# Attention start and emission order of a fused attention and two-layer feed-forward kernel: rms_g by rows, batch 0's softmax in halves, fill products by a sliding span, a seeded plan

## The chip, the cores and the metric

The kernel runs on one core of a Trainium2 chip. The metric is the device time of one launch in microseconds (us), as the median of several runs. Engine names are those of the profile: PE is TensorE's matrix products, PEld its weight loads, DVE is VectorE, ACT is ScalarE, POOL is GpSimd, SP is the queue that issues most transfers. L557 is line 557 of the kernel before.

## The reference

The inputs are q, k, v of shape (4, 8, 576, 64), phi of shape (4, 8, 576, 32), and the weights of two feed-forward blocks; the weights are float64 and are taken apart bit by bit in the kernel. All results are float32-accurate.

```
a   = exp(phi - max over the 576 positions);  a /= sum over the positions + 1e-9
k_m = a^T k ;  v_m = a^T v                     # per batch and head, 32 x 64
p   = softmax(q k_m^T / 8) ;  x = p v_m        # 2304 tokens x 512
xn  = x / sqrt(mean(x*x) + 1e-6) * rms_g
h   = (silu(xn @ w_gate) * (xn @ w_val)) @ w_out          # 512 -> 1536 -> 512
out = act2(h @ w_in) @ w_out2                             # 512 -> 2048 -> 512
```

## The kernel before, in words

The kernel has three stages that overlap. First comes the attention over four batches. For each batch `soft` finds the maximum of phi over the positions, subtracts it and takes the exponential, and sums it; `memory` then contracts that with k and v (L578), divides by the sum (L597 is the product that adds the sums over the partitions, L607 to L624 the division) and transposes the small result (L632, L641: kmT, which the scores read). `pair` makes the scores (L694) and the softmax for two groups of 128 tokens at a time. Second comes the first feed-forward block: 24 pieces of 512 KB of the float64 weights are loaded to tiles called raw (L310) and converted to float32 by some five operations on DVE, ACT and POOL (`convert`, L310 to L346); `vw` folds v_m into them (L905), `gv` makes gate and value (L955), `out1` contracts with w_out (L1050). Third comes the second block as a fast matrix product with seven sub-products (L1393 and L1516).

In `soft` the maximum is found as follows. `fold` halves the nine position groups by four operations (L500); a transpose on PE (L513) and a reduction on DVE (L518) give two columns of maxima, `gm`. DVE then multiplies the identity by them (L523, tile `dg`), and PE multiplies `dg` by a matrix of ones, `spread` (L530), so that every partition holds the maxima. DVE subtracts them from phi (L536, one operation on 1152 columns), and ACT takes the exponential (L543, one operation). For the sum, `fold` is called again, this time on POOL. Its scratch tile `half` has one buffer for all folds.

The loads of phi, k, v and q all go out from SP (L442, L449, L477), in the order of the list LOADS: phi and kv of batch 0, q of batch 0, phi and kv of batch 1, and so on. rms_g, 512 values, is loaded by POOL (L415) to the tile gT with one value per partition and column, so every value is a piece of 4 bytes. gT is read when a batch's v_m is scaled (L647).

The order of all instructions is written by a planner, the class `Agenda`. Each stream of work (a generator) yields steps with an engine and a duration in us that is written in the code, for example `yield "V", 1.35`. The planner keeps a model clock, always takes the step that can start first (ties go to the lower priority number), and emits its instruction. On the chip each engine runs its instructions in the emitted order. The model times thus decide the order, nothing else.

`heat` emits products of zeros (bf16, 512 columns, L557) on PE, which the code calls heat and this document fill products. Their planned duration is 0.2133 us each. Before, the planner counts PE's work in fixed ticks of 3.413 us and adds fill products late in each tick until the tick holds 2.09 us; one bank, number 4, is theirs, and they end once the exponential of batch 2 is done, `('e', 2)`.

Of the kernel before, what the change touches and what calls it, by code (L numbers as in the profile page):

```python
# [1 line left out]

# [12 lines left out]
P = 128  # L15
# [21 lines left out]

HEAT = (4, ('e', 2), 2.09, 0.34)

# [10 lines left out]
FETCH = (256, 63, 80.0, 6.1, 3.6, 80)  # L50
TICK = 3.413
WARM = 1.38
P_SOFT, P_PAIR, P_CONV, P_VW, P_GV, P_OUT1, P_W2, P_F2 = 0, 100, 800, 102, 850, 900, 3000, 4000
# [10 lines left out]
class Agenda:  # L64
# [11 lines left out]
    def __init__(self, room):  # L76
        self.room = dict(room)
        self.turn = {}
        self.ticks = {}
        self.flags = {}  # L80
        self.free = {"D": 1.7}
        self.given = {}
        self.issued = 5
        self.landed = {}
        self.now = 0.0
        self.port = 0.0
        self.done = 0.0
        self.live = []
        self.count = 0

# [14 lines left out]
    def _landed(self, n):  # L105
        return self.landed.get((n + FETCH[1]) // FETCH[0] - 1, 0.0)

    def _issue(self, n, at, t):
# [20 lines left out]
    def _start(self, x):  # L129
        kind, arg = x[3]  # L130
        at = x[4]
        if kind == "take":
            return (at, None) if self.room[arg] else None
        if kind == "pick":
            free = [z for z in arg if self.room["bank", z]]
            return (at, min(free, key=lambda z: self.given.get(z, 0.0))) if free else None
        if kind == "flag":
            return (max(at, self.flags[arg]), None) if arg in self.flags else None
        if kind in ("give", "rest"):
            return at, None  # L140
        if kind == "heat":
            at = max(at, self.free.get("P", 0.0), self._landed(self.issued))
            tick = int(at / TICK)
            need = HEAT[2] - self.ticks.get(tick, 0.0)
            if need <= 0:
                return (tick + 1) * TICK + 0.01, None
            slow = 1.0 if self.ticks.get(tick - 1, 0.0) > WARM else 2.0
            return max(at, (tick + 1) * TICK - (need + HEAT[3]) * slow), None
        times = arg if isinstance(arg, tuple) else (arg,)
        if kind[0] == "P":  # L150
            at = max(at, self._landed(self.issued))
        starts = [max(at + HOP.get(x[5] + e, HOP[e]), self.free.get(e, 0.0)) for e in kind[: len(times)]]
        bias = BIAS.get(kind, 0.0)
        took = [self._took(kind, e, t, s) for e, t, s in zip(kind, times, starts)]
        z = min(range(len(times)), key=lambda z: starts[z] + took[z] + (bias if z else 0.0))
        return starts[z], z

    def run(self, stop=None):
        while self.live and not (stop and stop in self.flags):
# [28 lines left out]
            elif kind == "heat":  # L188
                tick = int(at / TICK)
                value = self.ticks.get(tick, 0.0) < HEAT[2]  # L190
                if value:
                    slow = 1.0 if self.ticks.get(tick - 1, 0.0) > WARM else 2.0
                    self.ticks[tick] = self.ticks.get(tick, 0.0) + arg
                    done = at + arg * slow
                    done += self._issue(2, at, arg * slow)
                    self.free["P"] = done
            else:
                value = kind[z]
                t = self._took(kind, value, arg[z] if isinstance(arg, tuple) else arg, at)
                if value == "P":  # L200
                    tick = int(at / TICK)
                    slow = 1.0 if self.ticks.get(tick - 1, 0.0) > WARM else 2.0
                    self.ticks[tick] = self.ticks.get(tick, 0.0) + t * DUTY.get(kind.rstrip("0123456789"), 1.0)
                    t *= slow
                    t += self._issue(int(kind.lstrip("Pmsw")), at, t)
                done = self.free[value] = at + t
# [9 lines left out]
def tile_attn_moe(tc, q, k, v, phi, w_gate, w_val, w_out1, rms_g, w_in2, w_out2, out):  # L216
# [85 lines left out]
    def convert(src, pieces, dst, split, done, place=None):  # L302

        yield "take", "raw"
        yield "D", D_HALF
        n = nconv[0]
        nconv[0] += 1
        raw = wv.tile([P, CU, 2], U32, tag="raw", name=f"raw{n}", bufs=BUFS["raw"])
        rs = raw.rearrange("p n t -> p (n t)")
# [37 lines left out]
        yield "give", "raw"  # L347
        if split:
            if place:
# [77 lines left out]
    def loads():  # L427

        for s in LOADS:
# [8 lines left out]
            if s[0] == "phi":  # L438
                b = s[1]
                yield "Dq", 1.8  # L440
                t = phi_t[b] = ld.tile([P, 4, J, M], F32, tag="phi", name=f"phi{b}", bufs=BUFS["phi"])
                nc.sync.dma_start(out=t.rearrange("p c j m -> p c (j m)"), in_=by_half(phi[b], J * M))  # L442
            elif s[0] == "kv":
# [28 lines left out]
    def load_q(s):  # L472
        b = s[1]
        yield "take", "q"
        yield "Dq", 3.6
# [12 lines left out]
    def fold(name, x, to, op):  # L488

        kind, e, took = ("Vmax", nc.vector, (0.67, 0.4, 0.3, 0.3)) if op == ALU.max else (  # L490
            "G", nc.gpsimd, (1.24, 0.8, 0.48, 0.48)
# [3 lines left out]
        for n, (dst, y, z) in enumerate((  # L495
# [4 lines left out]
            e.tensor_tensor(out=dst, in0=y, in1=z, op=op)  # L500
        yield "give", "half"

    def soft(b):
# [19 lines left out]
        nc.vector.tensor_tensor(  # L523
            out=dg, in0=ident.unsqueeze(1).to_broadcast([P, 2, P]),
            in1=gm.unsqueeze(2).to_broadcast([P, 2, P]), op=ALU.mult,
        )
# [8 lines left out]
        yield "V", 1.35  # L535
        nc.vector.tensor_tensor(  # L536
            out=ph, in0=ph,
            in1=mv.rearrange("p (c m) -> p c m", m=M).unsqueeze(2).to_broadcast([P, 4, J, M]),
            op=ALU.subtract,
        )  # L540
        yield "give", m_bank
        yield "A", 1.16
        nc.scalar.activation(out=ph, in_=ph, func=AF.Exp)  # L543
        mark(("e", b))
# [3 lines left out]
        mark(("s1", b))  # L548

    def heat():  # L550

        yield "take", ("bank", HEAT[0])
        t = psum.tile([P, 512], F32, tag=f"b{HEAT[0]}", name="heat")
        while HEAT[1] not in agenda.flags:
            go = yield "heat", 0.2133
            if go:
                nc.tensor.matmul(  # L557
                    out=t.rearrange("p (x n) -> p x n", x=2), lhsT=zeros[:, 0:P],
                    rhs=zeros.unsqueeze(1).to_broadcast([P, 2, 256]), start=True, stop=True,
                    skip_group_check=True,  # L560
                )
        yield "give", ("bank", HEAT[0])

    s1_t = {}

    def memory(b):
# [6 lines left out]
        for j in range(J):  # L573
            yield "Pm32", 0.25
            for g in range(2):
# [17 lines left out]
        yield "flag", ("s1", b)  # L593
        yield "P8", 0.1
        for g in range(2):
# [42 lines left out]
        for z in range(2):  # L638
# [5 lines left out]
            )  # L644
        mark(("km", b))
        yield "V", 0.28
        nc.vector.tensor_tensor(  # L647
# [39 lines left out]
    def scores(pr, qT, scv, w):  # L687
        if pr[0] < B:
            for i in range(2):
                yield "Ps32", 0.65  # L690
                for c in range(2 * i, 2 * i + 2):
# [8 lines left out]
            return  # L700
        yield "Ps64", 0.85
        for c in range(4):
# [14 lines left out]
    def pair(n):  # L717
# [107 lines left out]
        y = st.tile([P, I], F32, tag="y", name=f"y_{name}", bufs=BUFS["e"])  # L825
        yield "G", 0.4
        nc.gpsimd.tensor_scalar(
# [50 lines left out]
    def vw():  # L878
# [7 lines left out]
        for group in VW:  # L886
# [11 lines left out]
            for z, (n, hi, lo, vps) in enumerate(got):  # L898
                yield "Pw64", 1.02 if z + 1 < len(got) else 1.25
                t = w_t.pop(n)  # L900
# [273 lines left out]
    order.enter_context(tc.manual_schedule())  # L1174
    add(0, loads())
    for b in range(B):
        add(P_SOFT + 2 * b, soft(b))
# [461 lines left out]
```

## Time and profile before

| | us |
|---|---|
| median of 3 runs | 775.58 |
| lowest and highest run | 775.37, 775.75 |
| the profiled execution, whole | 775.85 |
| its span in the trace | 774.1 |

Times in the trace are us from the start of the span. 1.75 us of the profiled execution lie around its span. In the views by stretches, `(x39)` is the number of instructions, PEclk the granted TensorE clock as a share of full speed, and the DMA share is the mean busy share of the core's 16 DMA engines (packets that overlap count twice, so it can pass 1). "issue" as a reason for a wait means that the profile shows nothing that was waited for.

### The profile page before, as it was taken

To read this page: it belongs to the slowest core of one execution; us is meant where nothing else is said; L and a number is where in the kernel's file an instruction comes from. 1 tells how busy PE (TensorE), PEld (TensorE's weight loads), DVE (VectorE), ACT (ScalarE), POOL (GpSimd) and SP (SyncE) were. 2 spreads that over 40 slices of the span, in tenths; PEclk is the share of its full clock that TensorE was granted. 3 is DMA by queue.
4 is the path that set the end of the run, shared out by engine and by line. 5 is a ranking of instruction groups with operands and counts; after the bars stand their busy time and mean duration, and the time that the engine had idled before them with its cause. 6 is when DMAs were issued, how large, how long until landed. Compare 5 with 4: busy or idle time off the path is not lost.

```text
span 774.1 us, 17215 instructions
## 1 busy us (share of the span) xinstructions
PE 759.8 (98%) x6383; PEld 701.4 (91%) x6383; DVE 618.9 (80%) x1250; ACT 466.5 (60%) x967; POOL 65.6 (8%) x89
## 2 busy tenths in 40 slices
PE   8999999999999999999999999999999999999997
PEld 4777798889889988988899999999999999999997
DVE  3799789998888776767788889985599895689963
ACT  1678877865565655646466668555476463565552
POOL 3546700000000000000000000000000000000000
PEclk9999999999999999999999999999999999999999
DMA  9994537788688765599547898888888878858875
GB/s 326 377 372 146 202 121 241 240 264 290 232 271 284 262 232 204 213 322 317 196 164 250 301 311 294 248 278 286 279 267 269 269 237 256 266 178 243 272 245 180
DMA packets 113395, 197.49 MB, mean 255 GB/s; under 512 B 10400, under 2 KB 41120, under 8 KB 113312
## 3 DMA queue, kind: packets, MB, share of 16 engines
q1 hardware_dynamic: 112896, 196.06, 76.2%
q8 instruction: 51, 0.84, 0.4%
q10 hardware_dynamic: 384, 0.33, 0.1%
q14 instruction: 32, 0.26, 0.1%
q0 software_dynamic: 32, 0.00, 0.1%
HBM read 151.26 MB, written 45.09 MB: 254 GB/s over the span
## 4 chain that ended last, share of the span: by engine, by line
PE 91%; DVE 4%; ACT 3%; issue 1%; POOL 1%; DMA 0%; DVEq 0%; POOLq 0%; ACTq 0%
PE ops L1050 19%; PE acc_b L1516 15%; PE qb L1393 13%; PE gps L955 10%; PE vps L955 10%; PE qc L1393 6%; PE acc_c L1516 6%; PE qa L1393 3%; PE vwps L905 3%; PE xp L815 1%; PE heat L557 1%; PE qps L743 1%; PE kvps L578 1%; DVE gg_A L1466 1%; ACT raw L328 1%
## 5 line engine op out<-in xcount | busy, mean ns | idle before, releaser
L1050 PE MATMUL ops<-ab,wo1h 128*128 128x512 f32 (+1 forms) x480 | 137.7, 372 | 0.2 <-ACT xs L1064 0.2
L1393 PE MATMUL qb<-xop,wr 128*128 128x384 f32 x576 | 111.1, 338 | 0.0
L1393 PEld LDWEIGHTS qb<-xop,wr 128*128 128x128 f32 x576 | 100.7, 188 | 0.3 <-ACT u L1355 0.3
L1050 PEld LDWEIGHTS ops<-ab,wo1h 128*128 128x128 f32 x480 | 84.7, 189 | 16.4 <-issue 3.7
L1050 PE MATMUL ops<-ab,wo1l 128*128 128x512 f32 (+1 forms) x240 | 88.5, 369 | 0.0
L1516 PE MATMUL acc_b<-wor,gg_A 128*128 128x256 f32 x648 | 79.6, 280 | 1.4 <-ACT gg_A L1464 0.8
L1516 PEld LDWEIGHTS acc_b<-wor,gg_A 128*128 128x128 f32 x648 | 78.2, 188 | 1.8 <-ACT gg_A L1464 1.0
L1355 ACT ACTIVATE u<-qb 128x384 f32<-128x384 f32 x72 | 35.1, 488 | 55.6 <-PE qb L1393 55.2
L1393 PE MATMUL qc<-xop,wr 128*128 128x384 f32 x288 | 58.3, 337 | 0.0
L1516 PE MATMUL acc_c<-wor,gg_S 128*128 128x256 f32 x432 | 53.0, 280 | 0.0
L1050 PEld LDWEIGHTS ops<-ab,wo1l 128*128 128x128 f32 x240 | 45.3, 189 | 7.8
L1516 PEld LDWEIGHTS acc_c<-wor,gg_S 128*128 128x128 f32 x432 | 52.2, 188 | 0.0
L1516 PE MATMUL acc_b<-wor,gg_S 128*128 128x256 f32 x432 | 52.0, 280 | 0.0
L1516 PEld LDWEIGHTS acc_b<-wor,gg_S 128*128 128x128 f32 x432 | 51.6, 188 | 0.0
L1393 PEld LDWEIGHTS qc<-xop,wr 128*128 128x128 f32 x288 | 50.9, 188 | 0.0
L328 ACT ACTIVATE raw<-raw 128x512 uint32<-128x512 uint32 x68 | 45.4, 672 | 0.0
L987 ACT ACTIVATE kvth<-gps 128x64 f32<-128x64 f32 (+2 forms) x100 | 29.0, 304 | 22.2 <-PE gps L955 21.7
L1021 ACT ACTIVATE ab<-kvth 128x512 fp32r<-128x512 f32 (+1 forms) x40 | 22.5, 566 | 30.6 <-PE ops L1050 30.6
L955 PE MATMUL gps<-late,vwh 128*128 128x288 f32 x192 | 39.6, 295 | 0.0
L955 PE MATMUL vps<-late,vwh 128*128 128x288 f32 x192 | 39.6, 295 | 0.0
L1026 DVE TENSOR_TENSOR ab<-kvth,ab 128x512 fp32r<-128x512 f32 (+1 forms) x39 | 24.9, 640 | 17.3 <-ACT ab L1021 17.1
L925 DVE TENSOR_TENSOR vwl<-vwps,vwh 128x512 fp32r<-128x512 f32 x48 | 32.5, 686 | 6.5 <-ACT vwh L923 6.5
(185 smaller groups left out, 1741.8 us busy)
## 6 DMA issues: line engine op xcount, KB each, us to landing
wr<-win_d SPq DMA_DIRECT2D x168, 256.0 KB, 3.7
wor<-wout_d SPq DMA_DIRECT2D x168, 256.0 KB, 3.3
raw<-in_moe_w_out_dram SPq DMA_DIRECT2D x28, 512.0 KB, 4.2
win_d<-wins SPq DMA_DIRECT2D x56, 256.0 KB, 4.2
wout_d<-wouts SPq DMA_DIRECT2D x56, 256.0 KB, 2.5
raw<-in_moe_w_in_dram SPq DMA_DIRECT2D x16, 512.0 KB, 5.2
raw<-in_moe_w_gate_dram SPq DMA_DIRECT2D x12, 512.0 KB, 5.1
raw<-in_moe_w_val_dram SPq DMA_DIRECT2D x12, 512.0 KB, 5.2
```

The costliest lines, as they stand in the source:

```text
L328: nc.scalar.activation(out=low, in_=low, func=AF.Copy, scale=LOW_SCALE, bias=LOW_BIAS)
L557: nc.tensor.matmul(out=t.rearrange("p (x n) -> p x n", x=2), lhsT=zeros[:, 0:P], rhs=zeros.unsqueeze(1).to_broadcast([P, 2, 256]), start=T ...
L905: nc.tensor.matmul(out=vps[g][0][32 * c : 32 * c + 32, 2 * P * x : 2 * P * x + 2 * P], lhsT=vT[n // NF1 * 2 + x][hs, c, :], rhs=t[hs, c].r ...
L925: nc.vector.tensor_tensor(out=lv, in0=vps[g][0], in1=hv.bitcast(F32), op=ALU.subtract)
L955: nc.tensor.matmul(out=p[:, 0:HB], lhsT=wt[:, g, i, :], rhs=at[b][:, g, c], start=(g == 0 and y == 0), stop=(g == 1 and y == 2),)
L987: nc.scalar.activation(out=t, in_=g[:, c], func=AF.Silu)
L1021: nc.scalar.activation(out=ah, in_=src, func=AF.Copy)
L1026: (nc.vector if eng == "V" else nc.gpsimd).tensor_tensor(out=al, in0=src, in1=ah.bitcast(F32), op=ALU.subtract)
L1050: nc.tensor.matmul(out=p[:, 0:n], lhsT=wt[:, fc, d], rhs=at, start=(fc == 0 and x == 0), stop=(fc == NF1 - 1 and x == 2),)
L1355: nc.scalar.activation(out=u, in_=src, func=AF.Copy)
L1393: nc.tensor.matmul(out=bank, lhsT=wt[:, kc, :], rhs=xt[:, kc, :], start=(start and kc == 0 and i == 0), stop=(kc == 1 and i == 2), skip_gr ...
L1516: nc.tensor.matmul(out=acc[x + "001"[t]][:, t % 2], lhsT=g[:, gi, P * t : P * t + P], rhs=w[:, wi], start=((o, t) in FIRST and q == 0 and ...
```

## The change

It does seven things.

1. rms_g is loaded to four rows of 128 values (`g4`), from ACT's queue, and a new stream `gains` transposes it on PE after the exponential of batch 0, and copies it to gT by DVE. `memory` waits for that before it scales v_m.
2. k of batch 0 is issued from ACT's queue instead of SP's.
3. `dg` and `spread` go. The product that spreads the maxima takes `gm`, broadcast to 64 columns, as its weights and the identity as its moving operand.
4. For batch 0 the subtraction and the exponential are done in two halves, so that the first exponential can start after the first half; the sum's fold of batch 0 is on DVE instead of POOL.
5. Fill products: the planner keeps a list of PE's work, and adds a fill product when the 3.413 us that end after it hold less than 2.0 us of work. They end with kmT of batch 3, `('km', 3)`, and each takes the bank that is free and was given back first.
6. Each planned duration is multiplied by a random factor between 0.97 and 1.03 from a seeded generator.
7. Several planned durations are changed, and a raw load waits in the plan until the buffer four loads earlier is given back.

```
-HEAT = (4, ('e', 2), 2.09, 0.34)
+HEAT = (('km', 3), 2.0, 0.2133, (4, 5, 6, 7, 0, 1, 2, 3))
+SEED, WOBBLE = 4, 0.06
+    def _active(self, end):
+        total, start = 0.0, end - TICK
+        for a, b, work in reversed(self.active):
+            if b <= start:
+                break
+            total += work * (min(b, end) - max(a, start)) / (b - a) if a < end else 0.0
+        return total
         if kind == "heat":
             at = max(at, self.free.get("P", 0.0), self._landed(self.issued))
-            tick = int(at / TICK)
-            need = HEAT[2] - self.ticks.get(tick, 0.0)
-            if need <= 0:
-                return (tick + 1) * TICK + 0.01, None
-            slow = 1.0 if self.ticks.get(tick - 1, 0.0) > WARM else 2.0
-            return max(at, (tick + 1) * TICK - (need + HEAT[3]) * slow), None
+            while self._active(at + HEAT[2]) >= HEAT[1]:
+                at += 0.1
+            free = [z for z in HEAT[3] if self.room["bank", z]]
+            return (at, min(free, key=lambda z: self.given.get(z, 0.0))) if free else None
...
                 t = self._took(kind, value, arg[z] if isinstance(arg, tuple) else arg, at)
+                t *= 1 + WOBBLE * (self.random() - 0.5)
...
     def convert(src, pieces, dst, split, done, place=None):
         yield "take", "raw"
-        yield "D", D_HALF
         n = nconv[0]
         nconv[0] += 1
+        if n >= BUFS["raw"]:
+            yield "flag", ("raw free", n - BUFS["raw"])
+        yield "D", D_HALF
...
-    nc.gpsimd.dma_start(out=gT, in_=rms_g.rearrange("(c p) -> p c", p=P))
+    g4 = st.tile([KC, P], F32, name="g4")
+    nc.scalar.dma_start(out=g4, in_=rms_g.rearrange("(c p) -> c p", p=P))
-    spread = st.tile([P, HP], F32, name="spread")
-    nc.gpsimd.memset(spread, 1.0)
...
                 for i, src in ((0, k), (1, v)):
-                    yield "Dq", 3.6
-                    nc.sync.dma_start(
+                    yield "Dq", 3.0 if b == 0 else 3.3
+                    (nc.scalar if (b, i) == (0, 0) else nc.sync).dma_start(
...
-        kind, e, took = ("Vmax", nc.vector, (0.67, 0.4, 0.3, 0.3)) if op == ALU.max else (
+        kind, e, took = ("Vmax", nc.vector, (0.67, 0.4, 0.3, 0.3)) if op == ALU.max or name == "s0" else (
             "G", nc.gpsimd, (1.24, 0.8, 0.48, 0.48)
...
+    def exp_phi(b, c, n):
+        yield "A", 0.12 + 0.26 * n
+        nc.scalar.activation(out=phi_t[b][:, c : c + n], in_=phi_t[b][:, c : c + n], func=AF.Exp)
+        mark(("e", b, c))
...
-        yield "Vdg", 0.42
-        dg = st.tile([P, 2, P], F32, tag="dg", name=f"dg{b}", bufs=BUFS["gm"])
...
-                out=mv[HP * g : HP * g + HP], lhsT=spread, rhs=dg[:, g], start=True, stop=True,
+                out=mv[HP * g : HP * g + HP], lhsT=gm[:, g : g + 1].to_broadcast([P, HP]), rhs=ident, start=True, stop=True,
...
+        n = 2 if b == 0 else 4
+        for c in range(0, 4, n):
+            yield "V", 0.08 + 0.318 * n
...
+            add(P_SOFT, exp_phi(b, c, n))
...
+    def gains():
+        yield "flag", ("e", 0)
+        gp, g_bank = yield from bank("t", "gps")
+        yield "P2", 0.1
+        nc.tensor.transpose(gp[:, 0:KC], g4, ident[0:KC, 0:KC])
+        yield "V", 0.2
+        nc.vector.tensor_copy(out=gT, in_=gp[:, 0:KC])
+        yield "give", g_bank
+        mark("gT")
```

The changed planned durations are: the phi load 1.8 to 1.6; k, v and q 3.6 to 3.0 (batch 0's k and v) or 3.3; L578 0.25 to 0.22; L597 0.1 to 0.35; L694 0.65 to 0.5 and L705 0.85 to 1.0; L905 1.02 and 1.25 to 0.9 and 1.1; L827 0.4 to 0.3.

## Rows read from the trace of the kernel before

**Rows 1.** The page, part 1: busy us of each engine, share of the span, instructions
```profile
PE 759.8 (98%) x6383; PEld 701.4 (91%) x6383; DVE 618.9 (80%) x1250; ACT 466.5 (60%) x967; POOL 65.6 (8%) x89
```

**Rows 2.** Busy time of the engines in six stretches: us, PE, PEld, DVE, ACT, POOL
```profile
0.00:12.30 12.30, 10.86 (x39) 4.16 (x39) 3.94 (x8) 2.45 (x2) 4.15 (x20) 1.00 0.86 285
12.30:37.40 25.10, 23.05 (x500) 18.32 (x500) 16.88 (x45) 13.47 (x28) 12.53 (x16) 1.00 1.06 383
37.40:92.00 54.60, 49.40 (x814) 39.95 (x816) 48.48 (x108) 46.03 (x101) 34.29 (x41) 1.00 0.68 236
92.00:200.00 108.00, 108.00 (x995) 95.62 (x987) 96.52 (x202) 74.94 (x174) 7.80 (x9) 1.00 0.71 234
200.00:700.00 500.00, 499.21 (x3486) 474.34 (x3471) 399.61 (x784) 296.03 (x597) 6.87 (x5) 1.00 0.78 257
700.00:740.00 40.00, 39.20 (x333) 39.03 (x332) 37.06 (x76) 20.63 (x41) 0.00 (x0) 1.00 0.82 258
```

**Rows 3.** The same view, PE's fill products alone
```profile
0.00:12.30 12.30, 10.49 (x34) 1.00 0.86 285
12.30:37.40 25.10, 3.28 (x12) 1.00 1.06 383
37.40:92.00 54.60, 0.38 (x1) 1.00 0.68 236
```

**Rows 4.** Timeline of the first 21 us: start, us, engine and line
```profile
6.21 0.29 DVE L500 TENSOR_TENSOR pm<-pm,phi 128x128 f32<-128x128 f32 x1
8.06 0.27 PE L513 MATMUL mps<-ident,pm 128*128 128x128 f32 x1
8.37 0.29 DVE L518 TENSOR_REDUCE gm<-mps 128x2 f32<-128x128 f32 x1 [1.87 <-PE mps L513]
9.25 0.44 PE L530 MATMUL mps<-dg,spread 128*64 128x128 f32 x4
9.74 1.35 DVE L536 TENSOR_TENSOR phi<-phi,mps 128x1152 f32<-128x1152 f32 x1 [0.54 <-PE mps L530]
11.13 1.16 ACT L543 ACTIVATE phi<-phi 128x1152 f32<-128x1152 f32 x1 [5.10 <-DVE phi L536]
12.35 2.25 PE L578 MATMUL kvps<-kv,phi 64*32 64x128 f32 x144 [0.39 <-ACT phi L543]
12.38 1.28 POOL L500 TENSOR_TENSOR halfs<-phi 128x512 f32<-128x512 f32 x1 [7.49 <-ACT phi L543]
15.03 0.69 DVE L500 TENSOR_TENSOR halfm<-phi 128x512 f32<-128x512 f32 x1 [3.94 <-POOL s L500]
16.09 0.39 PE L597 MATMUL kvps<-consts,s 64*128 64x1 f32 x4 [0.96 <-POOL s L500]
20.28 0.38 ACT L641 ACTIVATE kmT<-kT 64x256 f32<-64x256 f32 x1
```

**Rows 5.** DMA issues by window of issue: KB each, us to landing
```profile
phi<-in_phi_dram SPq DMA_DIRECT2D x1, 576.0 KB, 3.9
kv<-in_v_dram SPq DMA_DIRECT2D x1, 1152.0 KB, 9.9
gT<-in_moe_rms_g_dram POOLq DMA_DIRECT2D x1, 2.0 KB, 6.9
kv<-in_v_dram SPq DMA_DIRECT2D x1, 1152.0 KB, 15.1
```

**Rows 6.** Timeline of the queues: when three of these were issued
```profile
0.72 0.46 SPq L442 DMA_DIRECT2D phi<-in_phi_dram  x1
1.77 0.51 SPq L449 DMA_DIRECT2D kv<-in_v_dram  x1
8.29 1.57 SPq L449 DMA_DIRECT2D kv<-in_v_dram  x1
```

**Rows 7.** Busy time in stretches of 1 us; the last number is GB/s
```profile
6.00:7.00 1.00, 1.00 (x5) 0.36 (x4) 0.47 (x2) 0.03 (x1) 0.00 (x0) 1.00 1.49 315
7.00:8.00 1.00, 1.00 (x6) 0.52 (x5) 0.00 (x0) 0.00 (x0) 0.00 (x0) 1.00 0.60 161
```

More of the change, by code (lines that the diff above doesn't have):

```diff
@@ L1 @@
 from contextlib import ExitStack
+from random import Random
 import concourse.bass as bass
@@ L83, in __init__ @@
         self.issued = 5
+        self.active = []
         self.landed = {}
@@ L88, in __init__ @@
         self.live = []
+        self.random = Random(SEED).random
         self.count = 0
@@ L189, in run @@
                 tick = int(at / TICK)
[L190 to L196, printed above, removed]
+                value = z
+                slow = 1.0 if self.ticks.get(tick - 1, 0.0) > WARM else 2.0
+                self.ticks[tick] = self.ticks.get(tick, 0.0) + arg
+                done = at + arg * slow
+                self.active.append((at, done, arg))
+                done += self._issue(2, at, arg * slow)
+                self.free["P"] = done
             else:
@@ L204, in run @@
                     t *= slow
+                    self.active.append((at, at + t, t * DUTY.get(kind.rstrip("0123456789"), 1.0)))
                     t += self._issue(int(kind.lstrip("Pmsw")), at, t)
@@ L347, in convert @@
         yield "give", "raw"
+        mark(("raw free", n))
         if split:
@@ L439, in loads @@
                 b = s[1]
-                yield "Dq", 1.8
+                yield "Dq", 1.6
                 t = phi_t[b] = ld.tile([P, 4, J, M], F32, tag="phi", name=f"phi{b}", bufs=BUFS["phi"])
@@ L474, in load_q @@
         yield "take", "q"
-        yield "Dq", 3.6
+        yield "Dq", 3.3
         t = q_t[b] = st.tile([P, 4, J, D], F32, tag="q", name=f"q{b}", bufs=BUFS["q"])
@@ L520, in soft @@
         )
-        yield "Vdg", 0.42
-        dg = st.tile([P, 2, P], F32, tag="dg", name=f"dg{b}", bufs=BUFS["gm"])
[L523 to L526, printed above, removed]
         yield "P8", 0.3
@@ L534, in soft @@
         yield "give", "gm"
[L535 to L540, printed above, removed]
+        n = 2 if b == 0 else 4
+        for c in range(0, 4, n):
+            yield "V", 0.08 + 0.318 * n
+            nc.vector.tensor_tensor(
+                out=ph[:, c : c + n], in0=ph[:, c : c + n],
+                in1=mv.rearrange("p (c m) -> p c m", m=M)[:, c : c + n].unsqueeze(2).to_broadcast([P, n, J, M]),
+                op=ALU.subtract,
+            )
+            add(P_SOFT, exp_phi(b, c, n))
         yield "give", m_bank
-        yield "A", 1.16
-        nc.scalar.activation(out=ph, in_=ph, func=AF.Exp)
+        for c in range(0, 4, n):
+            yield "flag", ("e", b, c)
         mark(("e", b))
@@ L548, in soft @@
         mark(("s1", b))
-    def heat():
[L552 to L562, printed above, removed]
+    def gains():
[7 more added lines that the diff above has]
+        mark("gT")
+    def heat():
+        while HEAT[0] not in agenda.flags:
+            z = yield "heat", 0.2133
+            t = psum.tile([P, 512], F32, tag=f"b{z}", name="heat")
+            nc.tensor.matmul(
+                out=t.rearrange("p (x n) -> p x n", x=2), lhsT=zeros[:, 0:P],
+                rhs=zeros.unsqueeze(1).to_broadcast([P, 2, 256]), start=True, stop=True,
+                skip_group_check=True,
+            )
     s1_t = {}
@@ L573, in memory @@
         for j in range(J):
-            yield "Pm32", 0.25
+            yield "Pm32", 0.22
             for g in range(2):
@@ L593, in memory @@
         yield "flag", ("s1", b)
-        yield "P8", 0.1
+        yield "P8", 0.35
         for g in range(2):
@@ L645, in memory @@
         mark(("km", b))
+        yield "flag", "gT"
         yield "V", 0.28
@@ L689, in scores @@
             for i in range(2):
-                yield "Ps32", 0.65
+                yield "Ps32", 0.5
                 for c in range(2 * i, 2 * i + 2):
@@ L700, in scores @@
             return
-        yield "Ps64", 0.85
+        yield "Ps64", 1.0
         for c in range(4):
@@ L825, in pair @@
         y = st.tile([P, I], F32, tag="y", name=f"y_{name}", bufs=BUFS["e"])
-        yield "G", 0.4
+        yield "G", 0.3
         nc.gpsimd.tensor_scalar(
@@ L898, in vw @@
             for z, (n, hi, lo, vps) in enumerate(got):
-                yield "Pw64", 1.02 if z + 1 < len(got) else 1.25
+                yield "Pw64", 0.9 if z + 1 < len(got) else 1.1
                 t = w_t.pop(n)
@@ L1175, in tile_attn_moe @@
     add(0, loads())
+    add(P_SOFT, gains())
     for b in range(B):
```

## Prediction

> **What bounds the kernel now.** I read the page's busy shares first: PE is busy for 759.8 of the 774.1 us of the span [rows 1], so the end moves only with PE's idle time, with work that PE does in vain, or with slower products. The second view cuts the span into stretches [rows 2] and shows where the idle time is: 1.44 us up to 12.3, 2.05 up to 37.4, 5.20 up to 92, nothing from 92 to 200, 0.79 from 200 to 700, 0.80 from 700 to 740. The third view takes the fill products out of the busy time [rows 3]: 10.49 us up to 12.3, 3.28 up to 37.4, 0.38 up to 92, 14.15 in all. So before 92 PE does no useful work for 8.69 + 14.15 = 22.8 us, and after 92 it is a queue that never runs dry. Whatever the change gains, it must gain before 92, by making that queue start earlier; after 92 it can save at most the 1.6 us just listed, and it can lose more.
>
> The fourth view is the timeline of the first 21 us, read as a chain [rows 4]. phi of batch 0 lands at 0.72 + 3.9 = 4.62 [rows 5, 6]; the maximum's fold ends at 6.50; its transpose starts only at 8.06, behind the twenty fill products that the plan put ahead of it; the reduction ends at 8.66, the spreading product starts at 9.25, the subtraction at 9.74, the exponential ends at 12.29. k and v need 2.25 us from 12.35, and then PE waits: the sum, folded on POOL from 12.38, lets L597 start only at 16.09. kmT is complete at 20.66, and the scores follow. The fold for batch 1 starts at 15.03, released by that same POOL sum, since both use the one `half` tile.
>
> Up to 37.4 the DMA engines are full (share 1.06) [rows 2]. From 37.4 to 92 DVE is busy 89% and ACT 84%: there the attention and the weight conversion share two engines, and this backlog sets when PE's queue is full.
>
> **The change, part by part.**
>
> *The head of batch 0, up to the exponential.* The transpose stays at 8.06: worked by hand from the code, the new fill rule plans twenty products ahead of it again (nine at the planner's slow rate up to 3.84, then eleven up to 7.5), so 0 gained; one product fewer would be about 0.2. Without `dg` the spreading product follows the reduction at about 8.7 instead of 9.25: -0.55. The subtraction of 1.35 becomes two of about 0.70 (half, plus some 0.03 for one more start), and the exponential of 1.16 two of about 0.62, the first of which lies beside the second subtraction: 0.70 + 0.70 + 0.62 instead of 2.51, -0.49. Together the exponential would end at 12.29 - 1.04 = 11.25.
>
> *Loads.* v of batch 0 lands at 1.77 + 9.9 = 11.67 [rows 5, 6], which would now be later than the exponential. But rms_g's load, 2 KB in 6.9 us [rows 5], lies over a hole in the traffic, 315 and 161 GB/s in 6 to 8 us [rows 7] against 383 in the full stretch [rows 2]: (68 + 222) KB missing, 0.76 us of traffic. Loaded as four rows it should take next to nothing. The profile does not show that rms_g makes the hole, so this term lies between 0 and -0.8; I take -0.4, since the hole lies inside its flight but an instruction fetch could make it too. v then lands at about 11.3, and L578 starts at 11.4 instead of 12.35: -0.95.
>
> *k on ACT's queue.* ACT has nothing to do before 4.6, so two issues cost it nothing. The bytes are the same, but they now run beside phi of batch 0 instead of behind it. Bounds: 0, and if they share evenly, phi's 576 KB take twice their 1.5 us at 383 GB/s: +1.5. The fold would then end at 8.0, still not after the 8.06 that the fill products set: I take 0. That cover is the fill products; without them all of it would show. The Trainium skill ("DMA: Bandwidth & Descriptors", on issuing engines that are not separate queues, and on queue arbitration) speaks against this part: transfers started by several engines run on the same 16 DMA engines, packet by packet in turn, and only issue time is saved. No row here has two loads on two queues that could show it; by that rule phi is the later by up to the 1.5, and the sum stays, as the cover holds.
>
> *The sum on DVE.* L578 ends at 11.4 + 2.25 = 13.65. The sum's fold on DVE takes about what the maximum's takes, 6.50 - 4.62 = 1.9 at most, from 11.3, and the copy of rms_g before it, bounded by 0 and the reduction's 0.29, ends it by 13.4 at the latest. So the column sum L597 starts at about 13.65 instead of 16.09: -2.4. What is late next is k and v, not the sum. DVE does this in idle time; over all batches it gains four `dg` of 0.42, 1.7, and gains 1.8 of work, so its load in the backlog does not change.
>
> *What follows.* The steps from the column sum to kmT (4.2 us) stay, so kmT comes at 18.2 instead of 20.66: -2.4. Batch 1's fold starts at 13.4 instead of 15.03 (-1.6), but v of batch 1 lands at 8.29 + 15.1 = 23.4 [rows 5, 6], and moves only with the traffic, by -0.4, at best -0.8. So one stream into the backlog is 2.4 earlier, the other 0.4 to 0.8. The scores of batch 0 are the first to load DVE and ACT, and between 12.3 and 37.4 DVE has 8.2 us idle [rows 2] in which moved work fits; I put the whole backlog, and so PE's full queue at 92, at **-2.0**, nearer to the first. Ends: -0.4 and -2.6.
>
> *Fill products to kmT of batch 3.* Up to 37.4 I count the same number as before; up to 92 PE is already busy for 49.40 of 54.6 us [rows 2], far above 2.0 in 3.413, so only few are added, into gaps. Bounds: fewer fills by half of the 3.28 us [rows 3], -1.6, and eight more at 0.23 that all delay, +1.8; I take 0.
>
> *Planned durations, random factors, the wait for raw buffers.* They emit a different order everywhere. No row prices an order. From below: all 5.2 us idle between 37.4 and 92 and the 1.6 after 92 [rows 2] cannot come back; half is the most that I grant, -3.4. From above: twice the idle that PE has after 92, +3.2. I take 0, about the middle.
>
> **The sum** is made against the profiled execution of 775.85 us (0.27 above the median): 775.85 - 2.0 = 773.85, for the median 775.58 - 2.0 = **773.6 us**. A difference of 0.2%, 1.55 us, is about what a measurement of this kernel tells from none: the borders are 774.0 and 777.1.
>
> **The rivals.**
>
> *The gain is lost on the way (774.6 to 775.4).* The head gains 2.4, but batch 1 waits for its v at 23.4, the loads behind it are just as full, and DVE and ACT wait for what comes then. For it: a DMA share of 1.06 up to 37.4. Against: later loads (phi of batch 2 on) are waited for less than the engines. End: between -0.2 and -1.0, no measurable change. By the page's rule named above k on ACT's queue adds to this, phi up to 1.5 late, which decides once the fold ends after 8.06; every microsecond beyond that is lost from the 2.4, so a phi of 6.1 with one fill product fewer still leaves over -2 at kmT.
>
> *The order recovers more (769.6 to 772).* With durations nearer to the chip's, the plan also closes some of the 5.2 us of gaps and drops part of the 3.28 us of fills before 92: -2.0 and another -2 to -4. For it: there is that much to have. Against: gaps there follow from waits on busy DVE and ACT.
>
> *The new order stalls PE's full queue (777.2 to 779).* After 92 PE takes its products in the emitted order, and the old order leaves it idle for only 1.6 us of 648 [rows 2]. A random factor moves products ahead of operands that DVE or ACT deliver late, in the stretches where DVE is busy for 37.06 of 40 us [rows 2]. Each such place costs all of PE's wait. It decides once the idle time after 92 is 3.6 us above today's: then -2.0 becomes +1.6.
>
> *The change does not do what it says:* the fill products still start the transpose at 8.06, so the earlier steps are real but the fill rule itself changes nothing; this is inside the forecast.
>
> **How the numbers follow.** The forecast's case gets 0.40, of which 0.05 ends within the border of 774.0; the lost gain 0.22, all within; the better order 0.19, faster; the stalls 0.19, slower. That gives 0.54 faster, 0.27 within 0.2%, 0.19 slower. The forecast's own range is 772.8 to 775.2. The range for 8 in 10 takes in the lost gain and most of both other cases: 769.8 to 777.4.
>
> **What would show it.** In the new profile: the transpose of batch 0's maximum at 8.0 or a little later; the second exponential's end near 11.3; L578 at 11.4 and L597 near 13.7, not 16.1; no hole at 6 to 8 us; phi of batch 0 landing after 4.6 but before 6.2; kmT complete near 18.2; PE without gaps from about 90; fill products between 13 and 15 us in all. The prediction is wrong if kmT comes at 18 and PE's queue still fills at 92, if v of batch 0 lands after 12.3, or if PE's idle time after 92 is more than 4 us.

## The result, and the profile after

The changed kernel takes 781.84 us (median of 6 runs, 781.32 to 784.62), the kernel before 775.76 beside it. It is slower by 6.1 us, 0.8%, where 2.0 us less was forecast and the range ended at 777.4. The ratio, over all runs, is 1.0088, with a 95% interval of 1.0071 to 1.0106; it is more than 0.8% because two of the six runs took 784.4 and 784.6, which no run here explains. The profiled execution has a span of 780.2 us, 6.1 more than before, so the trace shows the difference of the medians.

The first view is the busy time in stretches, as in [rows 2]; the columns are us, PE, PEld, DVE, ACT, POOL, the granted clock, the DMA share and GB/s.

```profile
0.00:12.30 12.30, 10.31 (x18) 1.92 (x19) 1.86 (x5) 1.28 (x1) 3.12 (x18) 1.00 0.87 311
12.30:37.40 25.10, 24.04 (x439) 14.52 (x438) 15.33 (x44) 8.73 (x16) 5.17 (x7) 1.00 0.95 344
37.40:92.00 54.60, 52.41 (x846) 42.70 (x845) 49.75 (x104) 48.45 (x107) 36.95 (x45) 1.00 0.69 233
92.00:200.00 108.00, 107.31 (x974) 94.76 (x973) 95.56 (x206) 74.60 (x174) 7.74 (x10) 1.00 0.66 223
200.00:700.00 500.00, 498.87 (x3477) 472.07 (x3476) 400.02 (x783) 292.12 (x589) 8.11 (x6) 1.00 0.78 259
```

The same view with the fill products alone, as in [rows 3]:

```profile
0.00:12.30 12.30, 10.31 (x18) 1.00 0.87 311
12.30:37.40 25.10, 10.88 (x26) 1.00 0.95 344
37.40:92.00 54.60, 1.14 (x3) 1.00 0.69 233
```

The sum rows of the view over the whole span, before and after:

```profile
sum 774.10, PE 759.84 PEld 701.35 DVE 618.88 ACT 466.54 POOL 65.64; mean PE 94.98 PEld 87.67 DVE 77.36 ACT 58.32 POOL 8.21
sum 780.20, PE 768.39 PEld 701.05 DVE 621.76 ACT 462.92 POOL 61.09; mean PE 96.05 PEld 87.63 DVE 77.72 ACT 57.86 POOL 7.64
```

Up to 12.3 us PE does nothing but eighteen fill products, where the old kernel was already through the exponential of batch 0. In 12.3 to 37.4 the fills take 10.88 us instead of 3.28. All fills take 22.33 us instead of 14.15, with 46 of them instead of 47. PE's idle time falls from 14.26 us (774.1 - 759.84) to 11.81 (780.2 - 768.39), and its other work is the same within 0.4 us. So the difference is 8.2 us more of fills, 2.5 less of waiting and 0.4 of work, together the 6.1. Up to 92 us PE is idle for 5.24 us now and was for 8.69, so after 92 it is idle for 6.57 against 5.57: of the 6.1 us, 1.0 lies there, and the rest, 8.2 us of fills above all, lies ahead of it.

The third view is the timeline of the head; the rows answer to [rows 4]. Line numbers have moved: L534 is the old L513, L545 the old L530, L603 the old L578, L622 the old L597.

```profile
1.04 13.41 PE L583 MATMUL heat<-zeros 128*128 128x512 bf16 x21 [1.04 <-DVE zeros L435]
...
1.70 0.10 PEld L583 LDWEIGHTS <-zeros 128*128 128x128 bf16 x1 [0.54 <-issue]
...
6.43 0.29 DVE L516 TENSOR_TENSOR pm<-pm,phi 128x128 f32<-128x128 f32 x1
...
14.24 0.42 PE L534 MATMUL mps<-ident,pm 128*128 128x128 f32 x1
...
14.70 0.29 DVE L539 TENSOR_REDUCE gm<-mps 128x2 f32<-128x128 f32 x1 [7.98 <-PE mps L534]
...
15.65 0.70 PE L545 MATMUL mps<-ident,gm 128*64 128x128 f32 x4
...
17.19 1.35 ACT L521 ACTIVATE phi<-phi 128x576 f32<-128x576 f32 x2 [10.94 <-DVE phi L553]
...
19.50 2.25 PE L603 MATMUL kvps<-kv,phi 64*32 64x128 f32 x144
...
21.68 0.39 PE L622 MATMUL kvps<-consts,s 64*128 64x1 f32 x4
...
25.62 0.76 ACT L666 ACTIVATE kmT<-kT 64x256 f32<-64x256 f32 x2
```

The maximum is folded at 6.72, 0.2 later than before. Then its transpose waits until 14.24 behind twenty-one fills, which take 13.4 us. The row at 1.70 says how: each weight load of a fill comes after 0.54 us in which the engine waited for nothing that the profile shows. So the fills start 0.64 us apart (the next weight loads are at 2.34 and 2.98). Before, the twenty fills came 0.43 us apart at first and 0.22 later. The listing of PE's program, as it is built, shows the wait that the profile cannot name. This is its start in the changed kernel, where PE_49 is the counter (semaphore) of PE's own finished products:

```
1 L583 LDWEIGHTS zeros [waits DVE_49]
2 L583 MATMUL heat<-zeros 128x512
3 L583 LDWEIGHTS zeros
4 L583 MATMUL heat<-zeros 128x512 [waits PE_49]
5 L583 LDWEIGHTS zeros
6 L583 MATMUL heat<-zeros 128x512 [waits PE_49]
```

In the kernel before, none of the 47 fills waits so; here 42 of the 46 do. The reason is in the change. Every fill now takes a new tile, of the bank that was given back first. A fill never gives a bank back, so bank 4, which nobody uses this early, stays the one "given back first", and each new tile in it has to wait until the product that wrote the tile before has ended.

### The profile page after: what moved, and what is told of

The parts are those of the page before. It is cut to its first block, busy times and chain, and to the rows that moved or that the text cites. A ratio compares the mean times of both kernels' runs of the same rounds, so it can differ in the third digit from the quotient of the medians.

```text
span 780.2 us, 17231 instructions
## 1 busy us (share of the span) xinstructions
PE 768.4 (98%) x6383; PEld 701.0 (90%) x6383; DVE 621.8 (80%) x1257; ACT 462.9 (59%) x959; POOL 61.1 (8%) x84
## 4 chain that ended last, share of the span: by engine, by line
PE 94%; DVE 2%; ACT 1%; issue 1%; DMA 1%; SPq 0%; DVEq 0%; ACTq 0%
PE ops L1076 18%; PE acc_b L1543 16%; PE qb L1420 12%; PE gps L981 10%; PE vps L981 10%; PE qc L1420 6%; PE acc_c L1543 6%; PE qa L1420 3%; PE vwps L931 3%; PE heat L583 3%; PE xp L841 2%; PE kvps L603 1%; PE sc L720 1%; PE qps L769 1%; DMA x1B<-x_d 1%
## 5 line engine op out<-in xcount | busy, mean ns | idle before, releaser
L1013 ACT ACTIVATE kvth<-gps 128x64 f32<-128x64 f32 (+2 forms) x101 | 28.9, 305 | 18.4 <-PE gps L981 18.2
L1491 ACT ACTIVATE gg_S<-gs 128x384 fp32r<-128x384 f32 x52 | 26.8, 522 | 17.5 <-PE acc_b L1543 8.5
```

Source lines behind the costliest of these rows:

```text
L1013: nc.scalar.activation(out=t, in_=g[:, c], func=AF.Silu)
L1491: nc.scalar.activation(out=t[:, 0], in_=src, func=AF.Copy)
```

## The experiments

In every short diff, lines of the changed kernel or of the kernel before are marked -, and the experiment's are marked +. The first three set the wait against the order.

**One tile for the fills.** This keeps the order of all instructions and takes the wait away.

```
+        owner[z] = None                     # in bank(), when another stream is given bank z
...
-            t = psum.tile([P, 512], F32, tag=f"b{z}", name="heat")
+            if owner.get(z) is None:
+                owner[z] = psum.tile([P, 512], F32, tag=f"b{z}", name="heat")
+            t = owner[z]
```

> The changed kernel with one edit: a fill product writes the tile of the fill product before it, as long as nothing else has been given its bank in between, instead of a new tile each time; the emission order is the same. Theory A (each new tile of one bank makes the fill product wait for the one before it, which stretches 0.43 us to 0.64 and holds batch 0's transpose back by 6 us): fills at 0.43 us and 0.22 us, transpose at 8.1 to 8.5, whole 772.5 to 775.0. Theory B (the seeded order, the changed durations or the later end of the fills cost the 6 us): 780 to 782, with the transpose early or not.

Measured: 773.66 us, ratio 0.9973 (0.9962 to 0.9983). The timeline of its head (L537, L548, L608, L627 and L671 are the old L513, L530, L578, L597 and L641), and its fills by stretch:

```profile
1.04 6.09 PE L588 MATMUL heat<-zeros 128*128 128x512 bf16 x21 [1.04 <-DVE zeros L438]
...
6.96 0.27 PE L537 MATMUL mps<-ident,pm 128*128 128x128 f32 x1
...
7.62 0.44 PE L548 MATMUL mps<-ident,gm 128*64 128x128 f32 x4
...
8.90 1.35 ACT L524 ACTIVATE phi<-phi 128x576 f32<-128x576 f32 x2 [2.78 <-DVE phi L556]
...
11.46 2.24 PE L608 MATMUL kvps<-kv,phi 64*32 64x128 f32 x144 [1.63 <-DMA kv<-in_k_dram]
...
13.63 0.39 PE L627 MATMUL kvps<-consts,s 64*128 64x1 f32 x4
...
16.94 0.75 ACT L671 ACTIVATE kmT<-kT 64x256 f32<-64x256 f32 x2
```

```profile
0.00:12.30 12.30, 8.31 (x30) 1.00 0.87 313
12.30:37.40 25.10, 3.49 (x13) 1.00 1.06 380
37.40:92.00 54.60, 1.14 (x3) 1.00 0.70 245
```

The twenty-one fills ahead of the transpose take 6.1 us instead of 13.4, all fills 12.94 us instead of 22.33. Theory A's time and its fill distances hold; the transpose comes at 6.96, earlier than the 8.1 to 8.5 expected (the last section says why). The kernel is now faster than the one before by 2 us.

**The wait alone, in the kernel before.**

```
-        t = psum.tile([P, 512], F32, tag=f"b{HEAT[0]}", name="heat")
         while HEAT[1] not in agenda.flags:
             go = yield "heat", 0.2133
             if go:
+                t = psum.tile([P, 512], F32, tag=f"b{HEAT[0]}", name="heat")
```

> The kernel before with one edit: a new tile in bank 4 for each fill product; order and number of fills as before. Theory A: fills 0.64 us apart, transpose of batch 0 near 13.5, whole 780 to 783. Theory B: 775.5 to 776.5.

Measured: 787.91 us, ratio 1.0146 (1.0123 to 1.0170); its profiled execution took 784.03.

```profile
1.04 12.77 PE L557 MATMUL heat<-zeros 128*128 128x512 bf16 x20 [1.04 <-DVE zeros L417]
...
13.61 0.42 PE L513 MATMUL mps<-ident,pm 128*128 128x128 f32 x1
...
23.34 0.39 PE L597 MATMUL kvps<-consts,s 64*128 64x1 f32 x4
```

The transpose is at 13.6, as expected, and the column sum at 23.34 instead of 16.09. The one line costs this kernel more than the 4 to 7 us that I had put on it. In the profiled execution it costs 8.1 us of span, and the fills take 22.25 us instead of 14.15, also 8.1, since those after the transpose are stretched too. The other three runs took 787.8 to 788.0, and what their 4 us more are is not shown.

**A new tile each time, but in another bank.**

```
-            return (at, min(free, key=lambda z: self.given.get(z, 0.0))) if free else None
+            return (at, min(free, key=lambda z: max(self.given.get(z, 0.0), self.heated.get(z, 0.0)))) if free else None
...
+                self.heated[z] = at
```

> The changed kernel with one edit: the plan notes when a fill product took a bank, so that the fills go round the eight banks instead of staying in bank 4; each still takes a new tile. Theory A (the wait is for the write before in the same bank): that write is long done, fills 0.43 and 0.22 us apart, whole as in the run that reuses the tile, within 1 us, 772.5 to 775.5. If a new tile costs the time by itself, whatever the bank: 780 to 782. Theory B: 780 to 782.

Measured: 773.66 us, ratio 0.9976 (0.9966 to 0.9986).

```profile
1.04 7.13 PE L585 MATMUL heat<-zeros 128*128 128x512 bf16 x21 [1.04 <-DVE zeros L437]
...
8.01 0.27 PE L536 MATMUL mps<-ident,pm 128*128 128x128 f32 x1
```

Of its 46 fills 24 still wait on PE's counter, but all except one of them for a count at least seven back, and the time is that of one tile. So the price is the wait for the product just before, not the tile. With the order the same in the changed kernel and in both runs at 773.66, these three experiments settle the slowdown.

**The head's edits alone.** This is the kernel before with parts 1 to 4 of the change, written as in the diff; the fill rule, the planned durations and the raw loads stay, and there are no random factors.

> The kernel before with the edits of the head alone: rms_g by rows and transposed, k of batch 0 on ACT's queue, no identity times maxima, batch 0 in halves and its sum on DVE; fill rule, durations, raw loads and order rule as before. Theory A with the forecast of the head: kmT of batch 0 complete at 18.2, whole 773.0 to 775.0. Rival (the gain is lost on the way, behind the loads or in the shared engines): kmT near 18, whole 775.2 to 776.2.

Measured: 780.17 us, ratio 1.0058 (1.0044 to 1.0071). Neither forecast of the whole was right. (In this kernel L608 is the old L597, and L652 the old L641.)

```profile
13.56 0.39 PE L608 MATMUL kvps<-consts,s 64*128 64x1 f32 x4
...
17.84 0.38 ACT L652 ACTIVATE kmT<-kT 64x256 f32<-64x256 f32 x1
```

The head does what was forecast: kmT is complete at 18.22, the forecast was 18.2. But the plan behind it is another one, and it loses far more than the 2.4 us gained. Two stretches of its busy time show a part of that:

```profile
43.00:46.00 3.00, 2.30 (x34) 1.62 (x42) 2.97 (x10) 2.14 (x5) 0.00 (x0) 0.84 1.05 393
46.00:49.00 3.00, 3.00 (x36) 1.82 (x29) 2.02 (x8) 1.22 (x3) 2.29 (x2) 0.59 1.06 402
```

PE was busy for 2.30 of 3 us there, and the granted clock fell to a mean of 0.84 and then 0.59 of full speed, between its levels of 2.4 and 1.2 GHz. That is 0.16 + 0.41 of 3 us, 1.7 us of clock lost. The profiled execution is 3.9 us longer than that of the kernel before, and PE is idle as long as there (14.29 us, 14.26 there): its fills take 0.6 us more and its other products 3.2, of which the 1.7 is one part. What makes up the rest is open.

**The sliding fill rule added to that.** The kernel of the last run with part 5 of the change, one tile for the fills; the diff is that of the change.

> The head edits alone plus the sliding fill rule with its end at kmT of batch 3 (tile reused); durations, raw loads and order rule as before. With the head edits alone the granted clock fell to 0.84 and 0.59 in 43 to 49 us, after 1.4 us of PE idle in the 6 us before, some 1.7 us lost. Theory C (that fall is what the longer fills are for): granted clock 1.00 throughout and 777 to 778.5. If the clock was all that lost the head's gain: 773 to 774.5. If fills do not matter after 37 us: 779.5 to 780.7 with the clock falling again.

Measured: 779.02 us, ratio 1.0042 (1.0027 to 1.0057). Theory C is wrong in its reason and half a microsecond off in its time: the clock fell again, and for longer. The third guess has the clock right and is as far off on the other side; by the ratios this run and the last (1.0058) cannot be told apart.

```profile
40.00:44.00 4.00, 1.29 (x41) 1.17 (x36) 3.77 (x5) 3.59 (x8) 3.96 (x4) 0.89 1.06 389
44.00:48.00 4.00, 3.40 (x24) 2.92 (x23) 1.91 (x9) 1.15 (x3) 2.51 (x3) 0.50 1.06 398
48.00:52.00 4.00, 3.85 (x46) 2.45 (x46) 4.00 (x10) 3.10 (x7) 1.31 (x2) 0.76 0.99 388
```

In 40 to 44 us PE was busy for 1.29 of 4 us while DVE, ACT and POOL were all nearly full, so it looks as if PE waited for their results. The rows say otherwise. The first line is the end of PE's stop, the second, from the view of the DMA queues in 41.2 to 44.7 us, the queue that the profile calls "instruction":

```profile
44.60 0.85 PE L728 MATMUL sc<-kmT,qr 64*64 64x32 f32 x11 [3.31 <-issue]
q8 instruction: 1, 0.02, 2.2%
```

PE stops from 41.29 to 44.60 within one group of 32 like products, after 21 of them, and its program has no wait there. One packet of 16 KB is on the instruction queue from 41.92 to 43.16. Counted in PE's records in the trace (weight loads, products and waits), the stop comes after the 1473rd, and so it does with the head's edits alone (1.25 us) and in the kernel before with seed 4 (2.54 us, below). After the 1217th, 256 earlier, PE stops with seed 2 (2.35 us) and seed 5 (1.50), in the run with one tile (1.52) and in the changed kernel (1.27). Each of these stops ends 1.2 to 1.5 us after such a packet. So what PE waits for is most likely its next instructions, while the loads fill the DMA engines (share 1.06); the profile does not name it, and no run here moves it. The fill rule does not fill this stop, and could not if it is the instructions that are missing.

**Other draws of the random factors.** Two are the run with one tile, with `SEED, WOBBLE = 2, 0.06` and `5, 0.06`; the third is the kernel before with seed 4's factors on its own planned durations:

```
+SEED, WOBBLE = 4, 0.06
...
                 t = self._took(kind, value, arg[z] if isinstance(arg, tuple) else arg, at)
+                t *= 1 + WOBBLE * (self.random() - 0.5)
```

> The changed kernel that reuses the fill product's tile, with seed 2 instead of 4: the same instructions in another emission order. If the order that the random factors draw hardly matters: 773.2 to 774.2, as with seed 4. If it is a term of its own size: anywhere between 771 and 780, with the same fill products (0.43 and 0.22 us apart) and the head within 0.5 us, and the difference in PE's idle time after 37 us.

> The same with seed 5. Order hardly matters: 773.2 to 774.2. Order is a term of its own: 771 to 780, and not the time of seed 2.

> The kernel before with the random factors of seed 4 alone. Order hardly matters: 775.2 to 776.2. Order is a term of its own: 772 to 781, more likely slower, since it is one draw beside a plan with its own durations.

Measured: 781.65 us (ratio 1.0072, 1.0056 to 1.0087) with seed 2, 784.27 (1.0118, 1.0098 to 1.0138) with seed 5, and 785.92 (1.0138, 1.0121 to 1.0155) for the kernel before with seed 4. Against the kernel that has the same products in a good order (773.66, and 775.89 beside these runs) that is 8.0, 10.6 and 10.0 us more, and above all the times expected. All three lose clock between 37 and 52 us. With seed 2:

```profile
37.40:40.00 2.60, 0.98 (x51) 0.79 (x51) 0.43 (x1) 1.46 (x3) 1.75 (x2) 1.00 1.05 381
40.00:44.00 4.00, 4.00 (x57) 3.43 (x56) 1.89 (x3) 1.15 (x2) 0.00 (x0) 0.57 1.07 392
```

PE is busy for 0.98 of 2.60 us (the stop of 2.35 us named above), and then runs at a mean granted clock of 0.57, 1.7 us lost in 4.

A draw changes more than the order. The model times do not decide the order alone, as the part on the planner says: they also choose the engine of a step that may run on either of two (`yield "VAhi", (0.45, 0.68)` is one), and the number of fills: DVE has 1257 instructions with seed 4, 1253 with seed 2 and 1254 with seed 5, and there are 46 fills against 50 and 50. So "the same instructions" holds for PE's products, not for all. Where PE's time goes in the profiled executions, in us:

| | span | PE idle to 92 | idle after 92 | fills | PE's other products |
|---|---|---|---|---|---|
| kernel before | 774.1 | 8.7 | 5.6 | 14.2 | 745.7 |
| changed, one tile (seed 4) | 771.7 | 7.2 | 5.6 | 12.9 | 746.0 |
| the same, seed 2 | 780.4 | 8.3 | 8.0 | 15.3 | 748.9 |
| the same, seed 5 | 782.4 | 9.1 | 8.8 | 14.6 | 750.0 |
| kernel before, seed 4 | 783.8 | 13.2 | 8.0 | 13.2 | 749.5 |

In each of the three bad plans PE is idle for 2.4 to 3.1 us more after 92 us, and its products take 2.9 to 4.0 us longer, of which the slower clock is a part. It is not the main part: two of the four runs with seed 2 show a mean granted clock of 1.00 and still took 779.83 and 781.08. A draw of 3% on the durations is worth more than everything that the head's edits can save. The changed plan without any random factor was not tried on the chip, and how seed 4 was chosen is not known.

**Prices at one order.** The last four keep the order of the run with one tile, so that each gives the price of one edit. They were taken beside a kernel before of 776.14 us, the run with one tile beside one of 775.65, so differences of a few tenths between the medians count only as far as the ratios (0.9973 for one tile) bear them out.

k of batch 0 back on SP's queue:

```
-                    (nc.scalar if (b, i) == (0, 0) else nc.sync).dma_start(
+                    nc.sync.dma_start(
```

> The changed kernel that reuses the fill product's tile, with k of batch 0 back on SP's queue; the plan is the same. If k's queue is worth nothing, as forecast: 773.2 to 774.2, phi of batch 0 at about 4.6 instead of 4.8, v of batch 0 later, L578's counterpart within 0.5 us. If the second queue costs phi or saves issue time that the path sees: more than 0.7 us away.

Measured: 773.16 us, ratio 0.9963 (0.9950 to 0.9975), the lowest median of all, though its interval overlaps that of the run with k on ACT's queue. Landing times of batch 0's k and v, first with k on ACT's queue (one tile), then on SP's:

```profile
kv<-in_v_dram SPq DMA_DIRECT2D x1, 1152.0 KB, 8.7
...
kv<-in_k_dram ACTq DMA_DIRECT2D x1, 1152.0 KB, 9.9
```

```profile
kv<-in_k_dram SPq DMA_DIRECT2D x1, 1152.0 KB, 6.5
...
kv<-in_v_dram SPq DMA_DIRECT2D x1, 1152.0 KB, 9.0
```

Issued at 1.33 and 1.23, the pair is complete at 11.2; on one queue it is issued at 1.23 and 1.76 and complete at 10.8, and the products of k and v (L608) start at 10.86 instead of 11.46. The second queue buys nothing and delays the pair by some 0.5 us in these two executions. One thing changes with it: with k off SP's queue, phi of batch 1 goes out from there at 1.76 instead of 2.31 and runs beside the pair; the run does not part this from the queue itself. The Trainium skill ("DMA: Bandwidth & Descriptors", section "Issuing engines are not separate DMA queues") says that transfers of all engines interleave on the same 16 DMA engines and only issue time is saved; this pair agrees.

The old load of rms_g in addition:

```
+    gx = st.tile([P, KC], F32, name="gx")
+    nc.gpsimd.dma_start(out=gx, in_=rms_g.rearrange("(c p) -> p c", p=P))
```

> The same kernel as the one that reuses the tile, with the old element-by-element load of rms_g issued from POOL in addition, to a tile that nothing reads. If that load makes the hole of 0.76 us in the traffic at 6 to 8 us: the hole is back, kv of batch 0 lands 0.4 to 0.8 later, the whole 773.9 to 774.6. If an instruction fetch made it: no hole, 773.4 to 773.9.

Measured: 775.07 us, ratio 0.9988 (0.9979 to 0.9997). The traffic in 6 to 8 us, and the landing times:

```profile
6.00:7.00 1.00, 1.00 (x4) 0.40 (x3) 0.58 (x2) 0.17 (x1) 0.00 (x0) 1.00 1.47 345
7.00:8.00 1.00, 1.00 (x7) 0.46 (x5) 0.00 (x0) 0.00 (x0) 0.00 (x0) 1.00 0.63 143
```

```profile
kv<-in_v_dram SPq DMA_DIRECT2D x1, 1152.0 KB, 10.2
...
kv<-in_k_dram ACTq DMA_DIRECT2D x1, 1152.0 KB, 11.2
...
gx<-in_moe_rms_g_dram POOLq DMA_DIRECT2D x1, 2.0 KB, 7.6
```

The hole is back (345 and 143 GB/s; 412 and 403 in the run with one tile), and k and v land 1.3 and 1.5 us later, more than expected. The whole is 1.4 us slower in the median, 1.2 by the ratios. So the load makes the hole, and 2 KB as 512 values of 4 bytes cost this kernel 1.2 to 1.4 us.

Fourteen fills ahead of the transpose instead of twenty-one, the plan unchanged:

```
             z = yield "heat", 0.2133
+            n += 1
+            if 14 < n <= 21:
+                continue
```

> The same kernel as the one that reuses the tile, with 14 fill products ahead of batch 0's transpose instead of 21; the plan still counts 21. If the fills hold the transpose back on runs that warm up late: transpose at 6.6 to 7.0 always, whole 772.6 to 773.4. If the clock then falls: 774 or more, products after 7 us at half speed.

Measured: 774.57 us, ratio 0.9978 (0.9969 to 0.9987), slower by 0.9 in the median; by the ratios it cannot be told from the run with one tile. (L612 is the old L578.)

```profile
6.71 0.30 PE L537 MATMUL mps<-ident,pm 128*128 128x128 f32 x1 [0.45 <-DVE pm L519]
...
11.47 3.71 PE L612 MATMUL kvps<-kv,phi 64*32 64x128 f32 x144 [1.87 <-DMA kv<-in_k_dram]
```

```profile
12.00:15.00 3.00, 3.00 (x124) 0.50 1.06 392
15.00:18.00 3.00, 2.74 (x24) 0.93 1.05 392
```

The transpose is at 6.71, as expected, but the clock then falls: a mean of 0.50 in 12 to 15 us, and the 144 products of batch 0's k and v take 3.71 us instead of 2.24. This execution is the slowest of the eleven (775.16). The five with a mean granted clock of 0.998 took 774.64 to 775.16, the four with 1.000 took 773.41 to 774.07, which is the time with twenty-one fills. So seven fills fewer gain nothing where the clock holds, since k and v land no earlier, and cost some 1.1 us in the executions where it falls.

No fills after the exponential of batch 2:

```
             z = yield "heat", 0.2133
+            if ("e", 2) in agenda.flags:
+                continue
```

> The same kernel as the one that reuses the tile, without the 3 fill products planned after the exponential of batch 2. If the longer end of the fills keeps the clock in this order: a granted clock under 1.00 somewhere in 37 to 92 us and 774.5 to 777. If this order keeps PE busy enough by itself: 773.3 to 774.0 and 1.00 throughout.

Measured: 773.66 us, ratio 0.9965 (0.9953 to 0.9978), a granted clock of 1.00 throughout. In this order the three late fills do nothing that the runs can show.

## Why the prediction was wrong

**The step that failed** is the first: "The transpose stays at 8.06: worked by hand from the code, the new fill rule plans twenty products ahead of it again ..., so 0 gained". The count was right but for one (twenty-one). What I did not look at is what one of them costs: I priced a fill by the rows of before, where all fills write one tile, and passed over the line that gives each its own tile in the same bank. The runs put 8.2 us on it (781.84 against 773.66): 7.3 ahead of the transpose, which comes at 14.24 instead of 6.96, and the rest in the later fills. Of the 7.3 the wait itself is 21 times 0.21, 4.4 us; in the other 2.9 the fills after the seventh still run at their slow distance, where with one tile they had become fast. The bounds of the term on the fills, -1.6 to +1.8, were made of their number alone, and no rival had a transpose that comes late.

**A second step had no ground**, the order: "No row prices an order ... I take 0, about the middle", with bounds of -3.4 and +3.2. For seed 4 the sum came out with 0 in that place, but three other draws cost 8 to 11 us, and a new plan behind the head's edits took 4.5 although it had 2.4 in hand, so the bounds were far too narrow. The rival of stalls put the place after 92 us, in PE's full queue. In the bad plans 2.4 to 3.1 us of idle time are there; the rest lies before 92 and in products that take longer, and at 37 to 52 us PE stops and then loses its clock. The prediction says nothing of the clock, which the old trace shows at 1.00 in every stretch.

**What held, once the wait is gone** (the run with one tile): the reduction to the spreading product 0.05 us instead of 0.59, forecast -0.55; the column sum at 13.63, forecast 13.65; kmT complete at 17.69, forecast 18.2; k and v of batch 0 as the last thing waited for, landing at 11.2, forecast 11.3; 773.66 us, forecast 773.6. From the start of the subtraction to the end of the exponential it was 2.14 us (8.11 to 10.25), forecast 2.02; the 0.03 for one more start in that estimate stands on no row. Two of the agreements are luck. k and v land where they were forecast because two misses cancel: without rms_g's old load and with both on SP's queue they land at 10.8 instead of 11.67, 0.9 earlier and not 0.4, and k on ACT's queue takes 0.5 of it back. And the 773.6 proves less than it seems. The head's gain is real at kmT, but whether it reaches the end is decided by the order, and the run with the head's edits alone shows the opposite sign. How much of the 2 us is the head's and how much seed 4's is open, since every edit of the plan draws another order.

**Two smaller terms:** rms_g's load was taken at -0.4, with 0 and -0.8 as bounds; k and v land 0.9 us earlier without it and 1.3 to 1.5 later with it added back. k on ACT's queue was taken at 0, and delays the pair by about 0.5. Of the 1.5 us that an even sharing would have put on phi of batch 0, almost nothing came: its fold starts at 4.79 with k on ACT's queue and at 4.73 without.

## What to carry to other kernels

A product that takes a new tile of the bank that the product before it wrote waits for that product's end; give fill products one tile, or let them go round the banks. When the profile says only "issue", read the program's waits, and where the program has none, look for a packet on the instruction queue. A plan of this kind can answer a change of 3% in its durations with 10 us, so price an edit at a fixed order, and judge a plan by PE's idle time, the length of its products and the granted clock together. When fills stand ahead of real work, ask what one of them costs, not only how many there are.

## What was not expected of the hardware

While the fills came 0.64 us apart, with PE waiting in between, they stayed slow beyond the transpose: 584 ns each up to the one at 15.14 us, and 376 ns from 16.88. In the kernel before they fall from 634 to 380 ns at 6.55, with one tile at 3.94. The views show a granted clock of 1.00 in all these stretches, but the trace has no entry of it before 16.62, 6.53 and 3.88 us, which is where the fills become fast. So at the start of the span only the durations tell the two levels apart: I take the distances of 0.43 and 0.22 us for 1.2 and 2.4 GHz, twice the one being the other.

With fills back to back this moment differs between executions, and with it the transpose behind the same twenty-one fills: it came at 6.96, 8.01 and 8.45 us in three executions with this order, whose fills became fast at 3.94, 5.85 and 6.94. (The 8.06 of before, which the prediction kept, is such a draw too.) Their times agree within 0.4 us all the same, and the products of k and v start at 11.46, 11.46 and 11.48, because k and v land at about 11.2 in any case.
